# Tile loads issued as even and odd partitions, and one weight split moved ahead of another, in a retention and two-MLP kernel

## The chip, the cores and the metric

The kernel runs on one NeuronCore of a Trainium2 chip. The metric is the device time of one execution in microseconds (us), lower is better. A profiled execution gives the trace from which all rows below are read; its span runs from the first to the last instruction.

## The reference

Retention over 4 batches, 8 heads, 576 positions and head dimension 64, then two feed-forward blocks on the 2304 x 512 result, all in float32:

```python
scores = scale * np.matmul(q, k.transpose(0, 1, 3, 2))
ret = scores * Dmat[None, :, :, :]          # Dmat[h, i, j] = gamma[h] ** (i - j) for i >= j, else 0
attn_out = np.matmul(ret, v)
x = attn_out.transpose(0, 2, 1, 3).reshape(B * S, H * D)
...
h = x @ w_in;  x = np.maximum(h, 0.0) ** 2 @ w_out             # w_in 512 x 2048, w_out 2048 x 512
h = x @ w_in2; x = (h * np.clip(h + 3.0, 0.0, 6.0) / 6.0) @ w_out2
```

The four weight matrices come as 8-byte floats and are turned into 4-byte floats on the chip.

## The kernel before

**Retention.** The work is cut into ten units `u`: two pairs of batches, five blocks of positions each (four of 128, the last of 64). A unit of full width needs four tiles, two of queries and keys (`qkt`, from `in_qk`) and two of keys and values (`kvt`, from `in_kv`), each 128 partitions by 1024 floats, 512 KB. The last unit of a pair needs one tile from `in_qk_last` (512 KB) and two pieces of values of 128 KB, each 64 partitions wide: one goes to the lower 64 partitions of a tile, one to the upper (L271). Three pairs of tiles live in a buffer called `early`. So there are 16 + 16 whole tiles, two tiles from `in_qk_last` and four half-width pieces. Per unit, GpSimd (POOL) scales the keys (`scale_keys`, L283), TensorE (PE) makes scores (`aps`) and sums (`vps`, `sps`), VectorE (DVE) multiplies by the decay and writes the result into `xall` (L372).

**First feed-forward block.** For token group `pos` and chunk `c` of 128 hidden features, `emit_h` makes `hps` (24 matmuls where the group has 768 tokens, L439), ScalarE (ACT) and DVE make `g`, and `y_steps`, two chunks later (`LAG`), adds `g` times the chunk of w_out into `yps` and `ytail` (L497). A chunk of w_in reaches PE in three steps: load into `stage`, decode on ACT and DVE, and `split_in`, which makes a high part on ACT (L195) and a low part on POOL (L196) in a tile `win`. A chunk of w_out goes the same way into a tile `wo` (`split_out`). Each w_in chunk of this block is loaded in four pieces: 256 KB (L142), 128 KB (L144) and two of 64 KB (L145 and L146), the last two 64 partitions wide. The first two chunks of w_in are loaded between the tiles, chunks three to five and two chunks of w_out right behind the last tiles.

**Second block.** Its lines (L638 to L715) hold about half of PE's work and aren't touched.

**What sets the order.** The order in the program is written by hand, and each engine runs its instructions in that order. All loads of tiles and weights are issued by SyncE (SP), one after the other, in the order of the list `order` (built under `manual_schedule`); only the two loads of constants are issued by ACT. Eight completion semaphores, used in turn over SP's and ACT's loads, limit what is outstanding: a load waits until the load eight places ahead of it has landed. Tiles go to buffers that earlier tiles or steps leave free, so that some loads wait for PE or POOL as well.

The loop that the second part of the change touches runs over `i`, the pairs of `pos` and `c`: at `i` it emits `h` of chunk `i`, splits w_in of chunk `i + 2` (`split_in(*units[i + 2], ...)`, L931), splits w_out of chunk `i - 1` (`split_out(i - 1, ...)`, L933), and emits `y` of chunk `i - 2`.

Of the kernel before, what the change touches and what calls it, by code (L numbers as in the profile page):

```python
# [24 lines left out]
C = 128  # L25
# [50 lines left out]
def retention_moe_moe2(ctx, tc, qk, qk_last, kv, w_in, w_out, w_in2, w_out2, consts, out):  # L76

    nc = tc.nc
# [4 lines left out]
    NCH = DFF // 128  # L83
# [115 lines left out]
    def split_to(hi, lo, src, lo_engine):  # L199
        for f in split_parts(hi, lo, src, lo_engine):  # L200
            f()
# [8 lines left out]
    def unit(u):  # L210

        p, i = divmod(u, NTB)
        return 2 * p, i, min(C, S - C * i)
# [17 lines left out]
    def half(i):  # L231
        return slice(64 * i, 64 * i + 64)
# [3 lines left out]
    def space(u, k, which):  # L236

        b, i, n = unit(u)
        s = u // NTB * (2 * TILES + 1) + 2 * i + k
        if AHEAD <= s < AHEAD + WIDE:  # L240
            if not wide:
                wide.append(place("xr", [128, 2 * WIDE, 1024], F32, "early"))
            return wide[0][:, 2 * (s - AHEAD) + which]
        tags = TOKENS[s if s < AHEAD else (s - WIDE) % len(TOKENS)]
        name = ("qkt", "kvt")[which]
        if tags is None:
            return wop.tile([128, 1024], F32, tag="wo", name=name)
        return place(tags[which], [128, 1024], F32, name)

    def load_qk(u, k):  # L250
        b, i, n = unit(u)
        t = space(u, k, 0)
        if n == C:
            nc.sync.dma_start(out=t, in_=qk[b + k, i])
            data[u]["qk", k] = t.rearrange("p (e a t) -> p e a t", e=2, a=HP)
            return
        t = t.rearrange("p (b f) -> p b f", b=2)
        nc.sync.dma_start(out=t, in_=qk_last[b:b + 2].rearrange("b p e a t -> p b (e a t)"))
        for e in range(2):
            data[u]["qk", e] = t[:, e].rearrange("p (e a t) -> p e a t", e=2, a=HP)  # L260

    def load_kv(u, k):
        b, i, n = unit(u)
        t = space(u, k, 1)
        if n == C:
            t = t.rearrange("p (e h d) -> p e h d", e=2, h=H)
            nc.sync.dma_start(out=t, in_=kv[b + k, C * i:C * i + n])
            data[u]["k", k], data[u]["v", k] = t[:, 0], t[:, 1]
            return
        for e in range(2):  # L270
            nc.sync.dma_start(  # L271
                out=t[half(e), :H * D], in_=kv[b + e, C * i:, 1].rearrange("t h d -> t (h d)")
            )
        data[u]["v", 0] = t[:, :H * D].rearrange("p (h d) -> p h d", h=H)
# [112 lines left out]
    def split_x(pos, kk):  # L387
        t0, n = FIRST[pos]
        if pos == 0:
            if kk == 0:  # L390
                xtiles[0] = place("xr", [128, KD, 2, 768], F32R, "xring")
            hi, lo = (xtiles[0][:, kk, e] for e in range(2))
        elif (pos, kk) in ((3, 2),) or pos == 1:
            t = place("t7" if pos == 3 else ("x5", "x6", "t7", "ret")[kk], [128, 2, 512], F32R, "xown")
            hi, lo = (t[:, e] for e in range(2))
        else:
            if (pos, kk) == (2, 0):
                xtiles[2] = place("xr", [128, 2, 6, 512], F32R, "xring")
            slot = kk if pos == 2 else (4, 5, None, 0)[kk]
            hi, lo = (xtiles[2][:, e, slot] for e in range(2))  # L400
        xs[pos, kk] = hi, lo
        return split_parts(hi, lo, xall[:, kk, t0:t0 + n], nc.gpsimd if pos == 0 and kk in X_POOL else nc.vector)
# [8 lines left out]
    def wout_place():  # L411
        return wop.tile([128, 2, DM], F32R, tag="wo", name="wo")

    def split_out(c, lo_engine):
        w = wout_place()
        split_to(w[:, 0], w[:, 1], w32.pop((0, c, 1)), lo_engine)
        wouts[0, c] = w
# [12 lines left out]
    def emit_h(pos, c):  # L430
        w = wins.pop((pos, c))
        hs = []
        for k, (o, n) in enumerate(parts(pos)):
            own = pos == 0 or pos == 1 and c < LAG
            h = (bank(6 + (c % 2 if pos else k), [128, 512], "hps") if own else next_bank([128, 512], "hps"))[:, :n]
            m = 0
            for kk in range(KD):
                for wp, xp in PASSES:
                    nc.tensor.matmul(  # L439
                        out=h, lhsT=w[:, wp, kk * 128:kk * 128 + 128], rhs=xs[pos, kk][xp][:, o:o + n],  # L440
                        start=m == 0, stop=m == 3 * KD - 1,
                    )
                    m += 1
            hs.append(h)
        return hs
# [28 lines left out]
    def emit_g(pos, c, hs):  # L474
        relu, powers, low = g_steps(pos, c, hs)
        for k in range(len(relu)):
            relu[k]()
            powers[k]()
        for f in low:
            f()  # L480
# [270 lines left out]
    def next_load():  # L751

        turn["decoded"] += 1
        if coming and turn["decoded"] > 4:
            load_w(*coming.pop(0)[1:])

    with tc.manual_schedule():
# [88 lines left out]
        for u in range(UNITS):  # L846
# [6 lines left out]
            if u != 1:  # L853
                v = max(u - 1, 0)
                p = values(v)
# [7 lines left out]
        p = values(UNITS - 1)  # L863
# [16 lines left out]
        def opening(c, h, dec):  # L880

            relu, powers, low = g_steps(0, c, h)
            for f in dec[0]:
                f()
            next_load()
            for f in dec[1][:-1] if c == 0 else ():
                f()
            relu[0]()
            powers[0]()
            low[0]()  # L890
            if c == 0:
                dec[1][-1]()
                next_load()
            relu[1]()
            if c == 0:
                split_in(0, 2, nc.gpsimd)
            else:
                split_out(0, nc.vector)
            powers[1]()
            low[1]()  # L900

        for i, (pos, c) in enumerate(units):
            h = emit_h(pos, c)
            dec, due = due, []
            if i < 2:
                opening(i, h, dec)
                dec = []
            first = dec[:1]
            dec = dec[len(first):]
            for d in first:  # L910
                for f in d:
                    f()
                next_load()
            for d in dec:
                d.pop(0)()
            if pos and pos + 1 < len(FIRST) and c >= NCH - 3:
                for kk in ((0,), (1,), (2, 3))[c - NCH + 3]:
                    for f in split_x(pos + 1, kk):
                        f()
            if i > 1:  # L920
                emit_g(pos, c, h)
            for d in dec:
                for f in d:
                    f()
                next_load()
            if pos == 0 and c >= NCH - 3:
                for kk in ((0,), (1,), (2, 3))[c - NCH + 3]:
                    for f in split_x(pos + 1, kk):
                        f()
            if i and i + 2 < len(units):  # L930
                split_in(*units[i + 2], nc.gpsimd if i + 2 < NCH else nc.vector)  # L931
            if 2 <= i <= NCH:
                split_out(i - 1, nc.gpsimd)  # L933
            while halves and halves[0][0] <= i:
                d = decode(*halves.pop(0)[1:])
                d.pop(0)()
                due.append(d)
            if i >= LAG:
                for f in y_steps(*units[i - LAG]):
                    f()  # L940
                if i - LAG < NCH:
                    keep(("o", 0, i - LAG), wouts[units[i - LAG]].rearrange("p e n -> p (e n)"))
            if NCH <= i + 1 < len(units):
                load_out(0, *units[i + 1])
            if i in READY:
                owed += pace
                while ready and owed > ready[0][0] / 2:
                    cost, f = ready.pop(0)
                    f()
                    owed -= cost  # L950
            if pos == len(FIRST) - 1:
                if c == NCH - 5:
                    assert not ready
                    store_late()
                    load_left(0)
                if NCH - 5 <= c < NCH - 1:
                    for f in sums[2 * (c - NCH + 5):][:2]:
                        f()
                if c >= NCH - 3:
                    lows[c - NCH + 3]()  # L960
                if NCH - 4 <= c < NCH - 1:
                    highs[c - NCH + 4]()
# [13 lines left out]
        for k in range(total):  # L976
            j, p = divmod(k, NPAIR)
# [80 lines left out]
```

## Time and profile before

| | us |
|---|---|
| median of 3 runs (842.79 to 845.89) | 845.64 |
| the profiled execution's own time | 844.69 |
| its span | 842.9 |
| retention: from the start to the first `hps` matmul | 63.80 |
| PE busy in the whole span | 830.2 |

The span lies 1.8 us below the profiled execution's own time. In the page, engines are PE (matmuls), PEld (weight loads of TensorE), DVE, ACT, POOL and SP; SPq is SP's queue, where a load's row is its issue and not its transfer. "DMA share" is the mean busy share of the 16 DMA engines, and GB/s is what they moved.

### The profile page before, as it was taken

How to read it: one execution, taken by the hardware profiler on the slowest of the kernel's cores; microseconds unless marked ns; L12 is line 12 of the kernel's file. 1: busy time of each engine (PE TensorE's matmuls, PEld its weight loads, DVE VectorE, ACT ScalarE, POOL GpSimd, SP SyncE). 2: the span in 40 equal slices, each digit the busy share in tenths (PEclk: the TensorE clock that was granted, in tenths of full speed). 3: DMA queues.
4: the chain of work that ended last, by engine and by line, in shares of the span. 5: the costliest groups of instructions: out<-in, count | busy, mean ns of one | idle time of the engine just before them, and what ended most of it. 6: DMA issues, size and time to landing. Idle time of an engine off the chain costs nothing.

```text
span 842.9 us, 13274 instructions
## 1 busy us (share of the span) xinstructions
PE 830.2 (98%) x4932; PEld 721.6 (86%) x4932; DVE 524.6 (62%) x876; ACT 454.0 (54%) x847; POOL 142.9 (17%) x122
## 2 busy tenths in 40 slices
PE   8899999999999999999999999999999999999997
PEld 7788888888888888888888888898898889889896
DVE  5779777775777777687665644545644546534534
ACT  1247767676667877777665433345433345433332
POOL 2352323231432233333320000000000000000000
PEclk9999999999999999999999999999999999999999
DMA  9992556555778767877686464562864552854522
GB/s 361 366 324 70 189 177 199 177 191 190 262 265 311 250 240 264 307 277 251 225 290 246 171 218 163 176 211 89 310 227 163 190 197 89 331 208 160 205 95 76
DMA packets 67557, 183.47 MB, mean 218 GB/s; under 512 B 6818, under 2 KB 23586, under 8 KB 67492
## 3 DMA queue, kind: packets, MB, share of 16 engines
q1 hardware_dynamic: 66912, 181.82, 61.8%
q8 instruction: 39, 0.64, 0.3%
q10 hardware_dynamic: 580, 0.79, 0.3%
q14 instruction: 26, 0.21, 0.1%
HBM read 146.41 MB, written 36.18 MB: 217 GB/s over the span
## 4 chain that ended last, share of the span: by engine, by line
PE 85%; DMA 6%; DVE 2%; ACT 2%; issue 2%; POOL 1%; SPq 0%; ACTq 0%; DVEq 0%; POOLq 0%
PE yps L638 24%; PE hps L677 21%; PE hps L439 19%; PE yps L497 19%; DMA kvt<-in_kv_dram 4%; PE ytail L497 2%; DMA stage<-in_w_in_dram 2%; DMA cst<-in_consts_dram 1%; POOL wo L196 0%; POOL win L196 0%; DVE a L183 0%; ACT r L464 0%; ACT a L170 0%; ACT r L171 0%; DVE w L189 0%
## 5 line engine op out<-in xcount | busy, mean ns | idle before, releaser
L638 PE MATMUL yps<-wo,g 128*128 128x512 f32 x864 | 226.3, 394 | 0.0
L497 PE MATMUL yps<-g,wo 128*128 128x512 f32 x768 | 195.6, 392 | 1.0 <-POOL wo L196 1.0
L638 PEld LDWEIGHTS yps<-wo,g 128*128 128x128 f32 x864 | 159.7, 188 | 23.5 <-DVE g L692 0.3
L497 PEld LDWEIGHTS yps<-g,wo 128*128 128x128 f32 x768 | 140.0, 188 | 28.8 <-POOL wo L196 4.4
L439 PE MATMUL hps<-xring,win 128*128 128x512 f32 (+1 forms) x720 | 153.4, 362 | 0.9 <-DVE xall L372 0.9
L439 PEld LDWEIGHTS hps<-xring,win 128*128 128x128 f32 x720 | 123.2, 189 | 22.0 <-DVE xall L372 1.0
L677 PE MATMUL hps<-xlast,win 128*128 128x384 f32 x576 | 116.2, 336 | 0.0
L677 PEld LDWEIGHTS hps<-xlast,win 128*128 128x128 f32 x576 | 103.3, 188 | 8.8
L696 DVE TENSOR_TENSOR u<-hps,u 128x384 f32<-128x384 f32 x48 | 26.8, 558 | 107.3 <-PE hps L677 107.3
L468 DVE TENSOR_TENSOR g<-r,g 128x512 fp32r<-128x512 f32 x64 | 48.6, 760 | 69.5 <-ACT g L465 69.1
L677 PE MATMUL hps<-xop,win 128*128 128x384 f32 x432 | 87.2, 336 | 0.0
L461 ACT ACTIVATE r<-hps 128x512 f32<-128x512 f32 x80 | 43.9, 549 | 73.5 <-PE hps L439 73.4
L690 ACT ACTIVATE g<-c 128x384 fp32r<-128x384 f32 x72 | 37.8, 525 | 84.3 <-DVE c L689 84.3
L677 PEld LDWEIGHTS hps<-xop,win 128*128 128x128 f32 x432 | 77.5, 188 | 6.6
L688 ACT ACTIVATE v<-c,three 128x384 f32<-128x384 f32 x72 | 44.4, 617 | 32.7 <-DVE c L696 31.4
L439 PE MATMUL hps<-xown,win 128*128 128x512 f32 x240 | 59.7, 390 | 0.0
L195 ACT ACTIVATE win<-w 128x512 fp32r<-128x512 f32 x64 | 39.6, 619 | 26.8 <-DVE w L189 26.8
L715 ACT ACTIVATE c<-hps 128x384 f32<-128x384 f32 x24 | 11.8, 492 | 76.4 <-PE hps L677 76.4
L439 PEld LDWEIGHTS hps<-xown,win 128*128 128x128 f32 x240 | 44.9, 188 | 9.2
L174 DVE TENSOR_SCALAR a<-a 128x512 f32<-128x512 f32 x64 | 38.0, 594 | 23.0 <-ACT a L170 23.0
L464 ACT ACTIVATE r<-r 128x512 f32<-128x512 f32 x80 | 47.2, 590 | 2.5
L689 DVE SCALAR_TENSOR_TENSOR c<-v,c 128x384 f32<-128x384 f32 x72 | 40.0, 555 | 13.4 <-ACT v L688 13.4
(94 smaller groups left out, 983.0 us busy)
## 6 DMA issues: line engine op xcount, KB each, us to landing
wo<-kept SPq DMA_DIRECT2D x96, 512.0 KB, 5.0
win<-kept SPq DMA_DIRECT2D x72, 512.0 KB, 3.6
kept<-ready SPq DMA_DIRECT2D x40, 512.0 KB, 4.0
stage<-in_w_out_dram SPq DMA_DIRECT2D x32, 512.0 KB, 4.1
kept<-wo SPq DMA_DIRECT2D x16, 512.0 KB, 5.0
stage<-in_w_in_dram SPq DMA_DIRECT2D x16, 512.0 KB, 4.0
qkt<-in_qk_dram SPq DMA_DIRECT2D x13, 512.0 KB, 8.1
kvt<-in_kv_dram SPq DMA_DIRECT2D x13, 512.0 KB, 8.4
```

The source lines that it names most:

```text
L174: nc.vector.tensor_scalar(out=a, in0=a, scalar1=LEAST, scalar2=MOST, op0=ALU.max, op1=ALU.min)
L195: lambda: nc.scalar.activation(out=hi, in_=src, func=ACTF.Copy),
L439: nc.tensor.matmul(out=h, lhsT=w[:, wp, kk * 128:kk * 128 + 128], rhs=xs[pos, kk][xp][:, o:o + n], start=m == 0, stop=m == 3 * KD - 1,)
L461: relu.append(lambda r=r, h=hs[k]: nc.scalar.activation(out=r, in_=h, func=ACTF.Relu))
L464: nc.scalar.activation(out=r, in_=r, func=ACTF.Square)
L468: low.append(lambda r=r, hi=hi, lo=lo: nc.vector.tensor_tensor(out=lo, in0=r, in1=hi.bitcast(F32), op=ALU.subtract))
L497: nc.tensor.matmul(out=p, lhsT=w[:, wp, m * 128:m * 128 + 128], rhs=g[pos, c][k][:, gpart, :size], start=c == 0 and e == 0 and not (k and ...
L638: nc.tensor.matmul(out=p, lhsT=gt[m // 3][:, gpart, m % 3 * 128:][:, :128], rhs=w[:, wp], start=first and e == 0, stop=last and e == 2,)
L677: nc.tensor.matmul(out=to, lhsT=wl[k][:, half, wp, o], rhs=x[:, xp, f], start=first and m == 0, stop=last and m == 5, skip_group_check=True,)
L688: nc.scalar.activation(out=v, in_=c, func=ACTF.Relu, bias=three)
L689: nc.vector.scalar_tensor_tensor(out=c, in0=v, scalar=6.0, in1=c, op0=ALU.min, op1=ALU.mult)
L690: nc.scalar.activation(out=hi, in_=c, func=ACTF.Copy)
```

## The change

Every tile from `in_qk`, `in_kv` and `in_qk_last` is loaded by two loads of 64 partitions each, first the even partitions, then the odd ones (128 partitions by 4 KB become twice 64 by 4 KB). The half-width pieces of values and the weights are loaded as before. In the loop of the first block, at `i == 2`, the split of w_out chunk 1 is emitted ahead of the split of w_in chunk 4, where it stood behind it; from `i == 3` on the order is the old one.

```diff
         if n == C:
-            nc.sync.dma_start(out=t, in_=qk[b + k, i])
+            for e in range(2):
+                nc.sync.dma_start(out=t[e::2], in_=qk[b + k, i, e::2].rearrange("p e a t -> p (e a t)"))
             data[u]["qk", k] = t.rearrange("p (e a t) -> p e a t", e=2, a=HP)
             return
         t = t.rearrange("p (b f) -> p b f", b=2)
-        nc.sync.dma_start(out=t, in_=qk_last[b:b + 2].rearrange("b p e a t -> p b (e a t)"))
+        for e in range(2):
+            nc.sync.dma_start(
+                out=t[e::2], in_=qk_last[b:b + 2, e::2].rearrange("b p e a t -> p b (e a t)")
+            )
...
         if n == C:
+            for e in range(2):
+                nc.sync.dma_start(
+                    out=t[e::2], in_=kv[b + k, C * i + e:C * i + n:2].rearrange("p e h d -> p (e h d)")
+                )
             t = t.rearrange("p (e h d) -> p e h d", e=2, h=H)
-            nc.sync.dma_start(out=t, in_=kv[b + k, C * i:C * i + n])
...
+            if i == 2:
+                split_out(1, nc.gpsimd)
             if i and i + 2 < len(units):
                 split_in(*units[i + 2], nc.gpsimd if i + 2 < NCH else nc.vector)
-            if 2 <= i <= NCH:
+            if 3 <= i <= NCH:
                 split_out(i - 1, nc.gpsimd)
```

SP's queue at the start of the program, before; the names behind "waits" are the eight completion semaphores:

```order
L254 DMA qkt<-in_qk_dram 128x1024 x2
L267 DMA kvt<-in_kv_dram 128x1024 x2
L254 DMA qkt<-in_qk_dram 128x1024 x2
L254 DMA qkt<-in_qk_dram 128x1024 [waits DMAHW0_49]
L254 DMA early<-in_qk_dram 128x1024 [waits DMAHW1_49]
L267 DMA kvt<-in_kv_dram 128x1024 [waits DMAHW2_49]
```

The same place after the change:

```order
L255 DMA qkt<-in_qk_dram 64x1024 x4
L271 DMA kvt<-in_kv_dram 64x1024 x2
L271 DMA kvt<-in_kv_dram 64x1024 [waits DMAHW0_49]
L271 DMA kvt<-in_kv_dram 64x1024 [waits DMAHW1_49]
L255 DMA qkt<-in_qk_dram 64x1024 [waits DMAHW2_49]
```

Six loads are still issued before the first wait, but they are now three tiles instead of six, and the order of the tiles is the old one.

POOL's queue at the start of the first feed-forward block, before (`w_1002` holds w_in chunks 2 and 3, `w_1124` chunks 4 and 5):

```order
L196 TENSOR_TENSOR win<-w_1002,win 128x512 x2
L196 TENSOR_TENSOR win<-w_1124,win 128x512
L196 TENSOR_TENSOR wo<-wd,wo 128x512
L196 TENSOR_TENSOR win<-w_1124,win 128x512
L196 TENSOR_TENSOR wo<-wd,wo 128x512
```

The same place after the change, where the two buffers are called `w_1036` and `w_1158`:

```order
L196 TENSOR_TENSOR win<-w_1036,win 128x512 x2
L196 TENSOR_TENSOR wo<-wd,wo 128x512
L196 TENSOR_TENSOR win<-w_1158,win 128x512 x2
L196 TENSOR_TENSOR wo<-wd,wo 128x512
```

The low part of w_out chunk 1 has moved ahead of that of w_in chunk 4; on ACT, the two high parts have changed places in the same way.

## Rows read from the trace of the kernel before

**Rows 1.** The page's busy times of PE, and DMA in 40 equal slices of the span:

```profile
PE 830.2 (98%) x4932; PEld 721.6 (86%) x4932; DVE 524.6 (62%) x876; ACT 454.0 (54%) x847; POOL 142.9 (17%) x122
...
DMA  9992556555778767877686464562864552854522
GB/s 361 366 324 70 189 177 199 177 191 190 262 265 311 250 240 264 307 277 251 225 290 246 171 218 163 176 211 89 310 227 163 190 197 89 331 208 160 205 95 76
```

**Rows 2.** Waits up to 64 us: who for whom, us in total, times, longest:

```profile
POOL kvt L283 <- DMA kvt<-in_kv_dram: 27.7, 12, 8.0
```

**Rows 3.** The chain that ended last, up to 57 us (start, us, what):

```profile
6.56 11.17 DMA kvt<-in_kv_dram
...
49.50 7.08 DMA kvt<-in_kv_dram
```

**Rows 4.** The timeline behind the last tile: start, us, engine, line:

```profile
56.31 1.04 POOL L283 TENSOR_TENSOR kvt<-kvt,cst 128x512 f32<-128x512 f32 x1 [0.57 <-DMA kvt<-in_kv_dram]
...
63.80 13.02 PE L439 MATMUL hps<-xring,win 128*128 128x512 f32 x72 [0.88 <-DVE xall L372]
```

**Rows 5.** Stretches of retention; the last two numbers are DMA share and GB/s:

```profile
4.00:24.00 20.00, 18.50 (x330) 16.12 (x329) 13.40 (x23) 2.88 (x9) 7.80 (x7) 1.00 1.03 408
24.00:34.00 10.00, 8.21 (x218) 7.60 (x216) 4.38 (x9) 3.49 (x10) 3.06 (x4) 1.00 1.03 321
34.00:46.00 12.00, 10.78 (x208) 9.75 (x206) 11.94 (x22) 2.72 (x6) 4.70 (x4) 1.00 1.03 408
46.00:62.00 16.00, 15.03 (x355) 13.83 (x352) 11.19 (x17) 7.64 (x19) 10.35 (x9) 1.00 1.01 306
```

**Rows 6.** SP's queue where whole tiles are issued: start, us of one issue:

```profile
10.14 0.33 SPq L267 DMA_DIRECT2D kvt<-in_kv_dram  x1
11.41 0.33 SPq L267 DMA_DIRECT2D early<-in_kv_dram  x1
```

**Rows 7.** The 64-partition pieces of L271: their issue, and the last two's time to landing:

```profile
L271 SPq DMA_DIRECT2D kvt<-in_kv_dram x4: 471/471/471, 25.8 to 50.2; - x4
...
49.50 1.19 SPq L271 DMA_DIRECT2D kvt<-in_kv_dram  x2
...
kvt<-in_kv_dram SPq DMA_DIRECT2D x1, 128.0 KB, 7.1
...
kvt<-in_kv_dram SPq DMA_DIRECT2D x1, 128.0 KB, 6.8
```

**Rows 8.** The start: the first two stretches, and when the seventh SP load is issued:

```profile
0.00:2.00 2.00, 0.94 (x5) 0.69 (x6) 0.17 (x2) 0.25 (x1) 0.21 (x4) 1.00 0.10 18
2.00:4.00 2.00, 2.00 (x11) 1.40 (x10) 0.00 (x0) 1.03 (x1) 0.00 (x0) 1.00 0.86 296
...
5.16 0.33 SPq L254
```

**Rows 9.** The page's DMA issues, whole span: KB each, median us to landing:

```profile
stage<-in_w_in_dram SPq DMA_DIRECT2D x16, 256.0 KB, 2.7
```

**Rows 10.** PE, POOL and ACT around the wait for w_out chunk 1:

```profile
85.04 0.63 PE L497 MATMUL yps<-g,wo 128*128 128x512 f32 x2
86.53 0.51 PE L497 MATMUL yps<-g,wo 128*128 128x512 f32 x1 [0.86 <-POOL wo L196]
...
90.37 4.33 PE L439 MATMUL hps<-xring,win 128*128 128x512 f32 x24
...
83.75 1.30 POOL L196 TENSOR_TENSOR win<-w,win 128x512 fp32r<-128x512 f32 x1 [6.51 <-ACT win L195]
85.01 1.46 POOL L196 TENSOR_TENSOR wo<-wd,wo 128x512 fp32r<-128x512 f32 x1
...
80.57 0.42 ACT L465 ACTIVATE gtail<-r 128x256 fp32r<-128x256 f32 x1
83.04 0.63 ACT L195 ACTIVATE win<-w 128x512 fp32r<-128x512 f32 x1 [2.06 <-DVE w L189]
...
79.19 0.69 DVE L189 CUSTOM_DVE_ANT_0 wd<-a,r 128x1024 uint16<-128x1024 uint16 x1
```

**Rows 11.** PE's waits from 63.8 us to the end:

```profile
PE yps L497 <- POOL wo L196: 1.0, 2, 0.9
```

## The prediction

> **What bounds the kernel now.** I read the page first. PE is busy 830.2 of 842.9 us, and in the 40 slices the DMA engines are full only in the first three, at 361, 366 and 324 GB/s [rows 1]. So there are two stages: retention, up to 63.80 us, in which the loads set the pace, and the rest, in which PE does. Both parts of the change lie at or before 87 us, so I then read that beginning alone.
>
> The waits up to 64 us show who waits: POOL, which scales the keys of every tile, waits 27.7 us for tiles [rows 2]. The chain of waits says the same: up to 57 us it runs over loads, up to 11.17 and 7.08 us at a time [rows 3]. Behind the last tile the way is short and fixed: POOL scales its keys at 56.31, and the first `hps` matmul starts at 63.80, 7.5 us later [rows 4]. Once that matmul has started, PE hardly stops again: its only named waits to the end beside the one that starts it are 1.0 us on `wo` [rows 11]. So what the last tile's landing loses or gains goes through to the end nearly whole.
>
> How fast are the loads? In the stretches that move whole tiles almost alone (4 to 24 and 34 to 46 us) the DMA share is 1.03 and the rate 408 GB/s. In the two stretches between and behind them the share is as full (1.03 and 1.01) but the rate is 321 and 306 GB/s [rows 5]. The loads that stand in these two and not in the others are the half-width pieces of values, and the w_in chunks with their 1 KB rows and their two 64-partition pieces. A full share at a lower rate means that the engines aren't starved but that each packet takes longer. A whole tile takes 1.27 us: SP issues one each time one has landed, at 10.14 and 11.41 us [rows 6], and 524,288 bytes at 408 GB/s are 1.285 us.
>
> **The change part by part.**
>
> *Twice the issues.* 32 tiles and two from `in_qk_last` become 68 loads, 34 more. A 64-partition load takes SP 0.47 us to issue [rows 7], against 0.33 for a whole tile [rows 6]. Two halves are 0.94 us, below the 1.28 us that their bytes need, so SP still waits for landings and not the other way round: nothing, while that cover holds. If SP came to be the bound (an issue of 0.64 us or more) each tenth above would cost 68 x 0.1 = 6.8 us. SP has no other work in this stage; what queues behind its waits are the weight loads, which keep their places.
>
> *Half the bytes outstanding.* Eight halves are 2.1 MB, 5.1 us at 408 GB/s. A 256 KB load with little beside it lands 2.7 us after its issue [rows 9]. 5.1 is above 2.7, so in the steady stretches the engines don't run dry, and the tiles land in the old order at the old rate. The queue is shorter, but in a queue that is never empty the last byte comes when all bytes ahead of it have been moved; a shorter queue is worth nothing in itself.
>
> *The start.* Here the queue does run thin. Six halves are issued before the first wait, 1.57 MB or 3.9 us. Data starts at about 1.8 us (18 GB/s in the first 2 us) and the constants come beside it, so these bytes last to about 6 us. The seventh load is issued when the constants have landed, at 5.16 us [rows 8], and its data follows about 1.1 us behind its issue, as the first load's did (0.7 to 1.8). That is a gap of 0.3 to 0.6 us: I take +0.5.
>
> *What a 64-partition load costs.* This term decides. The trace has no load of every other partition; it has loads of 64 neighbouring ones. The last two pieces of L271 were issued at 49.50 and 50.22 (49.50 + 1.19 - 0.47) and landed 7.1 and 6.8 us later, at 56.6 and 57.0 [rows 7]: 0.45 us apart for 131,072 bytes, where 408 GB/s would give 0.32. That is a factor of 1.4 per byte. The stretches give a far worse one: they lose 10 x (1 - 321/408) = 2.1 and 16 x (1 - 306/408) = 4.0 us, with 384 and 640 KB of 64-partition loads in them. Charged to these bytes alone, 6.1 us on 1.05 MB make a factor of 3.4, but the 1 KB rows of w_in share the blame. From below, a load of every other partition may cost nothing more, since it goes to both halves of the tile and its packets are the same 4 KB; a gain per byte is excluded, because the whole tiles already run at a full share.
>
> The tiles are 34 x 524,288 = 17.8 MB, 43.7 us at 408 GB/s. So the ends are +0 (factor 1.0), +17.5 (1.4) and, if the stretches were right, over +100. The nearest rows are L271's, loads of 64 partitions that come one behind the other like these. But those fill one half of the partitions, and the even ones both halves, so part of what slows them should fall away; I take 1.3, that is +13.1 us. All of it lies on the path, since POOL already waits for every tile.
>
> [...]
>
> *The split moved.* PE waits 0.86 us in front of the third `yps` matmul of chunk 1 for the low part of its `wo`. POOL made that part at 85.01, behind the low part of w_in chunk 4 at 83.75, whose high part ACT could only start at 83.04, after 2.06 us of waiting for DVE [rows 10]. The decoded w_out chunk is ready at 79.19 + 0.69 = 79.9. With the new order ACT makes its high part behind `gtail` (81.0 to 81.6) and POOL its low part by 81.6 + 1.46 = 83.1, before PE asks for it, behind the two matmuls that start at 85.04. The w_in chunk now comes second, but ACT can't start it before 83.04 in either order and PE starts that chunk's `hps` only at 90.37 [rows 10]. So -0.9 us, and next in line is nothing that PE names [rows 11].
>
> **Sum.** 844.7 (the profiled execution's own time, 0.9 below the median) + 13.1 + 0.5 - 0.9 = 857.4 us.
>
> **The rivals.** *No price for the halves* (factor 1.0 to 1.05). For it: every DMA engine keeps 4 KB packets, each pair of halves covers the same partitions as the tile did, and the queue holds nearly twice what its latency needs. Against it: the only 64-partition loads in the trace are dear. It gives 844.7 + 0.5 - 0.9 = 844.3, and up to 846.5 at factor 1.05.
>
> *The slow stretches heal.* The 6.1 us that the two stretches lose could come from engines that are far apart: with eight whole tiles queued, one engine may write pieces of 64 partitions while another still writes whole tiles, and the two hinder each other. With half the bytes in the queue they stand closer together. For it: the share is full, so something inside the packets is slow. Against it: the tiles would then have to be free of that themselves, and the 1 KB rows stay. If two thirds of it heal: 844.3 - 4 = 840.3. This one ends faster, and decides as soon as more than about 3.8 us of the 6.1 come back.
>
> *Much slower.* Should the halves hinder each other as the pieces in the stretches do, the factor is 1.6 and more: +26 us, 870 or above. It needs the even and odd loads to collide all the time and not only at their ends.
>
> **How the numbers follow.** 0.5% of the median is 4.2 us, about what a measurement of this kernel can tell from no change. Halves that cost 1.1 to 1.55 (848 to 868): 0.43. Much slower: 0.07. No price: 0.38. Healing: 0.12. The likeliest is the first, at 857.4; its own range is 848 to 868. Since cases of both signs hold the chance, the range reaches over "no price" and to the lower end of its neighbour: 842 to 868, which leaves out some 0.09 below and 0.07 above. Faster by over 0.5% (below 841.4): 0.10. Within 0.5%: 0.40. Slower: 0.50.
>
> **What would show it.** Right: in the changed kernel the stretch from 4 to 24 us runs at 300 to 350 GB/s at a full DMA share, tiles land about 1.7 us apart instead of 1.28, and the first `hps` matmul starts near 76 us. Wrong toward "no price": 400 GB/s or more there, and the first `hps` matmul within 1 us of 63.8. Wrong toward healing: that matmul before 61 us, and over 350 GB/s in the stretches that hold the weight pieces. A DMA share clearly below 1 in the middle of a tile stretch would mean that the queue runs dry or that SP can't issue fast enough, so that a term I cost at nothing was the dear one. The second part is right if the wait on `wo` before `yps` of chunk 1 is gone; it is wrong if `hps` of chunk 4 waits for its `win` instead.

## The result, and the profile after

The changed kernel takes 848.12 us (median of 6 runs, 847.45 to 850.53); six runs of the kernel before on the same chip have a median of 843.89. The ratio is 1.0051, with a 95% interval of 1.0032 to 1.0071: 4.2 us slower. I had forecast 857.4, 12.7 us above the 844.7 from which I counted, so the sign was right and the size three times too large, and the reasons were mostly wrong too.

The profiled execution (850.53 us) is the slowest of the six. Its page, to be read beside [rows 1]:

```profile
PE 834.3 (98%) x4932; PEld 724.8 (85%) x4932; DVE 525.9 (62%) x876; ACT 454.0 (53%) x847; POOL 143.2 (17%) x122
...
DMA  8895565656578768876877465463764462864532
GB/s 326 282 313 157 174 198 174 198 183 215 206 265 300 252 244 296 300 259 232 287 236 272 161 215 190 143 223 110 273 253 169 168 215 88 308 225 162 193 105 75
```

Of the three slices that were full before, two no longer are. The same five stretches as in [rows 5], and one more, since retention now ends later (last two numbers: DMA share, GB/s; the number ahead of them is the granted clock):

```profile
4.00:24.00 20.00, 17.94 (x264) 15.15 (x261) 9.70 (x16) 2.52 (x9) 5.61 (x6) 0.83 0.98 366
24.00:34.00 10.00, 10.00 (x259) 9.54 (x254) 6.56 (x12) 3.33 (x11) 4.45 (x6) 1.00 0.84 270
34.00:46.00 12.00, 7.42 (x144) 6.43 (x136) 9.56 (x17) 1.44 (x4) 0.92 (x1) 1.00 0.90 294
46.00:62.00 16.00, 15.95 (x327) 14.80 (x327) 9.12 (x14) 6.03 (x16) 7.47 (x7) 0.89 0.90 305
62.00:70.00 8.00, 6.68 (x170) 5.54 (x163) 7.84 (x12) 3.63 (x10) 6.77 (x7) 1.00 1.00 282
```

This isn't the picture that I had forecast. I expected a full share at a lower rate, engines busy with dear packets. Here the share itself falls: 0.84 to 0.90 from 24 to 62 us, where every stretch had 1.01 to 1.03 before. Part of the engines wait for work. And where the share is full, they move halves as fast as they moved tiles:

```profile
10.00:16.00 6.00, 6.00 (x52) 4.50 (x54) 1.23 (x2) 0.60 (x1) 1.64 (x2) 0.53 1.01 406
16.00:22.00 6.00, 6.00 (x122) 5.81 (x119) 5.59 (x10) 1.14 (x4) 2.08 (x2) 1.00 1.02 397
```

Who keeps them waiting stands in SP's queue. First its timeline at the start (start, us, line, number of issues), then the issue times of the tile loads by line (shortest/median/longest in ns), after, and the line that answers to them in the kernel before:

```profile
3.27 2.51 SPq L271 DMA_DIRECT2D kvt<-in_kv_dram  x4
5.83 4.11 SPq L255 DMA_DIRECT2D qkt<-in_qk_dram  x6
```

```profile
L255 SPq DMA_DIRECT2D qkt<-in_qk_dram x26: 472/588/1484, 0.7 to 48.7; - x26
...
L271 SPq DMA_DIRECT2D early<-in_kv_dram x6: 472/597/2644, 18.2 to 23.3; - x6
```

```profile
L254 SPq DMA_DIRECT2D qkt<-in_qk_dram x13: 327/337/1096, 0.7 to 36.3; - x13
```

Four halves start within 5.83 - 3.27 = 2.56 us, 0.64 each. A tile costs SP 1.28 us, the time that the DMA engines need for it. So SP hardly waits for landings any more, as the first rows of SP's waits up to 62 us show (before, then after: who for whom, us in total, times, longest):

```profile
SPq L267 <- DMA kvt<-in_kv_dram: 5.3, 5, 2.1
SPq L254 <- DMA qkt<-in_qk_dram: 3.0, 4, 1.1
SPq L267 <- DMA qkt<-in_qk_dram: 2.7, 3, 0.9
```

```profile
SPq L271 <- DMA kvt<-in_kv_dram: 3.6, 3, 2.8
SPq L255 <- PE aps L329: 1.2, 1, 1.2
SPq L145 <- DMA qkt<-in_qk_dram: 1.2, 1, 1.2
SPq L255 <- PE sps L353: 0.7, 2, 0.4
```

Before, the three largest are waits for landings, 11.0 us; now the landings that SP waits for are few, and waits for PE (a buffer still in use) have joined them. Behind it all, POOL waits for tiles for 36.7 us in the first 66 us, 27.7 us in the first 64 before [rows 2], and PE's first `hps` matmul starts at 69.76 instead of 63.80 [rows 4]:

```profile
POOL kvt L290 <- DMA kvt<-in_kv_dram: 36.7, 12, 13.2
```

```profile
69.76 10.63 PE L446 MATMUL hps<-xring,win 128*128 128x512 f32 x55
```

Those 5.96 us are the whole of the longer span, 848.7 - 842.9 = 5.8 us, in this execution; the medians differ by 4.2. The second part of the change did what it says and gained nothing: chunk 1's `yps` doesn't wait any more, chunk 2's does, for longer than chunk 1's did [rows 10]:

```profile
99.57 0.63 PE L504 MATMUL yps<-g,wo 128*128 128x512 f32 x2
101.43 0.50 PE L504 MATMUL yps<-g,wo 128*128 128x512 f32 x1 [1.23 <-POOL wo L196]
```

One more thing stands in this trace. PE idled for lack of tiles, and twice its granted clock fell behind such a stretch: to 0.53 from 10 to 16 us (above), after it had idled 1.60 us in front of 8.31, and to 0.57 from 46 to 50, after 4 us in which it was busy for 0.94:

```profile
42.00:46.00 4.00, 0.94 (x16) 0.88 (x16) 2.02 (x3) 0.00 (x0) 0.92 (x1) 1.00 0.94 338
46.00:50.00 4.00, 3.97 (x56) 3.70 (x54) 1.29 (x2) 0.15 (x1) 1.17 (x2) 0.57 0.86 285
```

### The profile page after: what moved, and what is told of

Its sections match the earlier page's. It is cut to its first block, busy times and chain, and to the rows that moved or that the text cites. A ratio compares the mean times of both kernels' runs of the same rounds, so it can differ in the third digit from the quotient of the medians.

```text
span 848.7 us, 13334 instructions
## 1 busy us (share of the span) xinstructions
PE 834.3 (98%) x4932; PEld 724.8 (85%) x4932; DVE 525.9 (62%) x876; ACT 454.0 (53%) x847; POOL 143.2 (17%) x122
## 4 chain that ended last, share of the span: by engine, by line
PE 91%; DMA 3%; SPq 1%; issue 1%; DVE 1%; ACT 1%; POOL 1%; POOLq 0%; ACTq 0%; DVEq 0%
PE yps L645 24%; PE hps L446 21%; PE hps L684 21%; PE yps L504 20%; DMA kvt<-in_kv_dram 2%; PE ytail L504 2%; PE vps L345 1%; PE aps L329 1%; DMA qkt<-in_qk_dram 1%; PE sps L353 0%; DMA stage<-in_w_in_dram 0%; PE vps L361 0%; SPq L255 0%; DVE w L189 0%; DVE g L475 0%
## 5 line engine op out<-in xcount | busy, mean ns | idle before, releaser
L722 ACT ACTIVATE c<-hps 128x384 f32<-128x384 f32 x24 | 11.8, 492 | 76.5 <-PE hps L684 76.5
```

## The experiments

My theory after this reading (theory A in the expectations): a half load's bytes cost nothing, but its issue does. SP needs as long for a tile as the DMA engines do, so after any delay it can't get ahead again, and with half the bytes queued a delay reaches the engines sooner. The rivals: the shorter queue alone (theory B), a cost of 64-partition loads as such (theory C), the moved split, the clock. The kernels and what they gave (differences of medians in us, to the kernel before on the same chip):

| kernel | us | difference | ratio, 95% interval |
|---|---|---|---|
| split_alone | 844.92 | +0.2 | 0.9998 (0.9990 to 1.0006) |
| halves_alone | 848.51 | +3.8 | 1.0038 (1.0025 to 1.0051) |
| column_halves | 845.19 | +0.5 | 1.0009 (1.0001 to 1.0018) |
| short_queue | 846.37 | +1.7 | 1.0022 (1.0014 to 1.0031) |
| pause_eight | 844.68 | 0.0 | 0.9998 (0.9988 to 1.0008) |
| pause_whole | 846.12 | +1.6 | 1.0021 (1.0012 to 1.0030) |
| column_pause | 848.64 | +4.0 | 1.0048 (1.0036 to 1.0061) |
| quarters | 887.43 | +42.9 | 1.0510 (1.0485 to 1.0534) |
| contiguous_halves | 871.56 | +27.0 | 1.0320 (1.0295 to 1.0346) |
| late_halves | 846.10 | +1.4 | 1.0018 (1.0009 to 1.0026) |
| split_all | 845.04 | +0.5 | 1.0005 (0.9995 to 1.0014) |
| merged_last | 846.43 | +1.8 | 1.0022 (1.0014 to 1.0031) |

**Which part.** The two parts apart. `split_alone` is the kernel before with the diff's last piece only, `halves_alone` has the other two.

> Whole tile loads as before; only the moved w_out split of chunk 1. Theory (the split is worth nothing): the changed kernel waited 1.2 us for wo once, a chunk later, where the kernel before waited 1.0 us in two parts, so this one gives 843 to 845, ratio 0.999 to 1.001, with the wait for wo at the next chunk. Rival (the split costs part of the 4.2 us that the change lost): 845.5 us or more. Rival of the prediction: 0.9 us gained, 843.0.

> Even and odd halves as in the changed kernel; the two weight splits in their old order. If all of the loss is the loads': 847.5 to 849 us, ratio 1.004 to 1.006, retention's end at 68 to 70 us, the two waits for wo of 1.0 us together back. If the moved split has a part in it: at least 1.5 us less than the changed kernel.

The split alone is worth nothing, and the wait has moved to the next chunk:

```profile
95.81 0.50 PE L497 MATMUL yps<-g,wo 128*128 128x512 f32 x1 [1.25 <-POOL wo L196]
```

The halves alone lose 3.8 of the 4.2 us, and the intervals overlap widely: the loss is the loads'. This run's trace also clears the clock. It was granted in full through retention, and the first `hps` matmul was still 5.5 us late, in the slowest of five executions:

```profile
4.00:24.00 20.00, 17.03 (x284) 14.52 (x283) 10.51 (x18) 2.88 (x9) 4.85 (x6) 1.00 0.96 344
24.00:34.00 10.00, 9.31 (x231) 8.49 (x231) 5.47 (x11) 2.73 (x8) 4.90 (x6) 1.00 0.88 299
34.00:46.00 12.00, 8.74 (x172) 7.54 (x166) 9.70 (x17) 1.54 (x4) 1.45 (x2) 1.00 0.95 311
46.00:62.00 16.00, 14.74 (x317) 12.76 (x313) 11.18 (x18) 6.76 (x18) 7.30 (x6) 1.00 0.97 333
62.00:70.00 8.00, 6.82 (x147) 5.73 (x148) 5.20 (x10) 2.78 (x7) 6.28 (x6) 1.00 0.96 279
```

```profile
69.25 11.06 PE L446 MATMUL hps<-xring,win 128*128 128x512 f32 x57
```

**The shorter queue by itself.** `column_halves` cuts each tile by columns. It has as many loads of as many bytes as the change, but 128 partitions in each:

```diff
-            nc.sync.dma_start(out=t, in_=kv[b + k, C * i:C * i + n])
+            for e in range(2):
+                nc.sync.dma_start(out=t[:, e], in_=kv[b + k, C * i:C * i + n, e])
```

> Two loads for a tile again, 256 KB each, but each of 128 partitions by 2 KB: as many issues and as few bytes outstanding as in the changed kernel. Theory A (SP's issue time): a 128-partition issue took 0.33 to 0.47 us before, so a pair takes 0.7 to 0.9 us of the tile's 1.28, SP gets ahead again after each delay, and the time is 844 to 845.5, with the DMA share at 1.0 from 10 to 24 and from 34 to 46 us. Theory B (half the bytes outstanding run out, whatever an issue costs): 847.5 to 849 with the share falling under 0.9 in the same places as in the changed kernel. Theory C (a load of 64 partitions is itself slow): as A, and the loads' landings are then 1.28 us a tile.

`short_queue` loads whole tiles and sends a load of one element behind each, which takes up every second of the eight completion semaphores, and so of the eight places among the outstanding loads:

```diff
+    def dot():
+        nc.sync.dma_start(out=dots[:, spot[0]:spot[0] + 1], in_=consts[:1, :1])
+        spot[0] += 1
...
             nc.sync.dma_start(out=t, in_=qk[b + k, i])
+            dot()
```

> Whole tile loads with a one-element load behind each, which takes every second of the eight places in the queue: four tiles outstanding at most (half the bytes), one long issue per tile (0.33 to 0.47 us) and a small one (estimate 0.1 to 0.3). Theory A (issue time): SP is far from bound, 844 to 846. Theory B (the bytes outstanding): 847.5 to 849, with the DMA share under 0.9 in several stretches of two microseconds between 22 and 60 us.

The column halves lose 0.5 us, far from 3.8. Their issue is cheap, and the DMA share is full where the change left it at 0.84 and 0.90 (issue times in ns, shortest/median/longest; then two stretches):

```profile
L255 SPq DMA_DIRECT2D qkt<-in_qk_dram x26: 327/402/1664, 0.7 to 44.3; - x26
```

```profile
24.00:34.00 10.00, 8.96 (x232) 8.24 (x228) 4.92 (x10) 3.43 (x10) 3.55 (x5) 1.00 1.05 318
34.00:46.00 12.00, 10.46 (x199) 9.44 (x199) 11.54 (x21) 2.72 (x6) 3.27 (x3) 1.00 1.00 353
```

So theory B, the shorter queue as the whole cause, falls. The column halves do have a small price of their own per byte: from 10 to 20 us, where both kernels move tiles at a full share, their 2 KB rows go at 390 GB/s and the whole tiles of before at 412 (before, then `column_halves`):

```profile
10.00:20.00 10.00, 8.67 (x178) 8.19 (x177) 6.84 (x12) 1.46 (x6) 2.08 (x2) 1.00 1.03 412
```

```profile
10.00:20.00 10.00, 9.69 (x189) 9.12 (x190) 7.58 (x13) 1.74 (x5) 3.30 (x3) 1.00 1.06 390
```

But `short_queue` came out above the range that theory A gave it, with 1.7 us. A tile and its small load took SP 0.33 and 0.29 us:

```profile
10.90 0.33 SPq L275 DMA_DIRECT2D kvt<-in_kv_dram  x1
11.28 0.29 SPq L239 DMA_DIRECT2D dots<-in_consts_dram  x1
```

That is far from binding, so the queue has a part in the loss, or else the small loads have one of their own, which no run sets apart. Why four whole tiles outstanding should be worse than eight halves of the same bytes, these runs don't tell.

**SP's time by itself.** Whole tiles and the full queue again, but SP is kept busy: a number of semaphore increments, which nobody waits for, stand behind each tile load. Eight make a tile cost SP about 0.8 us, sixteen make it 1.32.

```diff
+    def pause():
+        for _ in range(16):
+            nc.sync.sem_inc(tick, 1)
...
             nc.sync.dma_start(out=t, in_=qk[b + k, i])
+            pause()
```

> Whole tile loads, all eight places of the queue for data (4 MB outstanding), but sixteen semaphore increments on SP behind each tile load, which delay nothing but SP. The trace of before has two such instructions on SP 0.055 to 0.075 us apart, so SP needs about 0.33 + 16 x 0.06 = 1.3 us for a tile, as much as two half loads (2 x 0.64). Theory A (SP's time is the loss): 847 to 849 us, retention's end 3 to 5 us later, DMA share under 0.95 in stretches behind each long issue. Rival (the loss needs small loads or a short queue): 844 to 845.5, since the queue holds as many bytes as before.

> Whole tile loads, eight semaphore increments on SP behind each: 0.33 + 8 x 0.061 = 0.82 us of SP for a tile that the DMA engines take 1.28 us for. Theory A with a threshold (SP's time costs nothing until it nears the engines' time): 844 to 845.2. If SP's time costs in proportion (half of the 1.6 to 1.8 us that sixteen cost): 845.3 to 845.6.

SP's timeline with sixteen: two loads in 1.64 us, and 17.17 - 14.53 = 2.64 us for the pair, 1.32 a tile.

```profile
14.53 1.64 SPq L259 DMA_DIRECT2D early<-in_qk_dram  x2
17.17 0.33 SPq L274 DMA_DIRECT2D kvt<-in_kv_dram  x1
```

At 0.8 us of SP for a tile the loss is 0.0, at 1.32 it is 1.6: no cost in proportion, but a threshold somewhere between the two, where the engines' own 1.28 lies too. And 1.32 is 0.04 more than 1.28, so that 34 x 0.04 = 1.4 of the 1.6 us may be SP as the plain bound. 1.6 is less than the 2.5 to 4.5 that theory A had promised. SP's time alone isn't the whole loss either.

**Both together.** `column_pause` is the column halves with five increments behind each, so that a half costs SP about what an even or odd one did:

> The halves by columns (128 partitions by 2 KB) with five semaphore increments on SP behind each, which took 0.061 us each in the run with sixteen of them: 0.33 + 0.31 = 0.64 us of SP for a half, what an even or odd half costs it, and as few bytes outstanding, but no load of 64 partitions. If SP's time and the short queue together are the whole loss: the sum of their own losses, 0.8 and 1.8 us, to the 3.8 us of the even and odd halves, so 847 to 849. If loads of 64 partitions lose time of their own: 844.5 to 846.

```profile
18.35 1.00 SPq L277 DMA_DIRECT2D kvt<-in_kv_dram  x2
19.69 1.00 SPq L277 DMA_DIRECT2D early<-in_kv_dram  x2
```

```profile
24.00:34.00 10.00, 8.87 (x235) 8.52 (x237) 5.07 (x10) 2.83 (x9) 5.15 (x6) 1.00 0.92 321
34.00:46.00 12.00, 9.50 (x170) 8.74 (x166) 9.21 (x17) 1.44 (x4) 2.09 (x2) 0.86 0.89 302
```

Two halves start in 19.69 - 18.35 = 1.34 us, 0.67 each, the share is down again as in the changed kernel, and the loss is 4.0 us, that of `halves_alone` (3.8). So a loss of this size needs no tile load of 64 partitions. The dose isn't quite the same: 0.67 is 0.03 more than an even or odd half costs SP, 68 x 0.03 = 2.0 us, but the engines, too, need 262,144 bytes / 390 GB/s = 0.67 us for a column half. In both kernels SP has nothing to spare; that the two losses are equal to a microsecond isn't shown.

The parts lost 0.5 and 1.6 us alone (0.8 and 1.8 by the ratios, as in the expectation) and 4.0 together. By the ratios the excess over the sum is some 1.5 us, and known to about as much. So that the two causes support each other, since a slow SP can't fill the queue again and a short queue can't cover a slow SP, is my reading and likely, but not shown; the runs show that the two together make a loss of the right size.

**What the delays are.** The traces show two kinds, which my theory had not named. In all fourteen traces together, 64 of SP's issues that start before 110 us took over 0.85 us. During 63 of them the queue that the page calls `q8 instruction` had one of its 16 KB packets on the way, but during only 125 of the 1392 shorter ones. The longest is the one of 2.64 us in the changed kernel (SP's timeline; then that queue from 23.4 to 25.7 us: packets, MB, share):

```profile
23.26 2.64 SPq L271 DMA_DIRECT2D early<-in_kv_dram  x1
```

```profile
q8 instruction: 1, 0.02, 6.1%
```

The kernel before has such an issue too, of 1.10 us at 28.27, but it issues a tile in 0.33 us and has the rest of 1.28 to make up for it. What the packet has to do with SP is not shown. The other kind is a load whose last part comes late. SP's longest wait for a landing after the change, 2.8 us up to 44.94, is for the half issued at 37.04: fourteen of its sixteen landing records are in by 42.34, the last comes at 44.92. All that time eight halves were outstanding, and from 42 to 43 us the DMA share was 0.83: some engines stood idle while that part was on its way. That a single engine lagged behind the others is my reading; the landing records don't name engines.

**More of the same dose.** Four loads of 32 partitions for a tile (`t[e::4]`):

> Four loads for a tile, every fourth partition each (32 partitions, 128 KB); the weight splits in the old order. Theory A with an issue of 0.47 to 0.6 us whatever its partitions: 4 x 0.55 = 2.2 us of SP for a tile of 1.28, so SP sets the pace: 34 tiles x 0.9 = 31 us more, 870 to 880, with a DMA share near 0.6. If the issue's time falls with the partitions (0.3 us): 848 to 850. If only the bytes outstanding count (a quarter of before): 850 to 856, with SP waiting for landings.

```profile
L271 SPq DMA_DIRECT2D kvt<-in_kv_dram x52: 527/592/1335, 5.8 to 99.0; - x52
```

```profile
4.00:24.00 20.00, 13.26 (x152) 10.25 (x150) 7.57 (x13) 1.74 (x5) 2.56 (x3) 0.87 0.63 198
```

An issue of 32 partitions takes as long as one of 64, 0.59 us, so 4 x 0.64 = 2.56 us for a tile and 34 x (2.56 - 1.28) = 43.5 us more; 42.9 were measured, in two runs. My expectation had been lower by its 0.55 us for an issue. Here SP is the bound outright.

**Which 64 partitions.** The halves as partitions 0 to 63 and 64 to 127 (`t[64 * e:64 * e + 64]`):

> The halves are partitions 0 to 63 and 64 to 127 in place of even and odd ones; the weight splits in the old order. If a load's partitions don't matter to its speed: as even and odd halves alone, 847.5 to 849.5. If the 64 neighbours take 1.3 times as long per byte, the term that the prediction put on even and odd ones: 43.7 us x 0.3 = 13 us more, 858 or so, with stretches at a share of 1.0 and 300 GB/s.

```profile
4.00:24.00 20.00, 16.83 (x168) 13.19 (x165) 8.49 (x16) 1.74 (x5) 2.99 (x3) 0.88 1.03 233
```

27 us slower, twice what the dear one of my two cases gave, and now with the picture that I had forecast for the change: a full share, 233 GB/s instead of 408. That is a factor of 1.75 per byte for 64 neighbours, against 1.0 for even and odd partitions. At 233 GB/s the 17.8 MB need 76.5 us instead of 43.7, and 27 of these 33 us reach the end; where the other 6 went stays open.

**Start or later.** The first eight tiles whole, halves from the third unit on (`if u < 2` keeps the old call):

> Whole loads for the eight tiles of the first two units, even and odd halves from there on; the weight splits in the old order. If the loss is made at the start, where the first kvt landed 1.8 us later: 844.5 to 846. If it is made behind the delays later on, when SP can't catch up: 847 to 848.5.

```profile
4.00:24.00 20.00, 18.88 (x336) 16.46 (x335) 13.67 (x23) 2.89 (x9) 7.64 (x7) 1.00 1.01 398
24.00:34.00 10.00, 9.42 (x228) 8.52 (x224) 5.65 (x13) 3.55 (x10) 3.24 (x5) 1.00 0.96 311
34.00:46.00 12.00, 8.94 (x178) 7.95 (x176) 9.19 (x16) 2.72 (x6) 3.19 (x3) 1.00 0.88 302
```

It loses 1.4 us, between the two expectations. So some 3.8 - 1.4 = 2.4 us (each of the two known to about 1) are lost because the first eight tiles are halved, while SP sends them at the very pace at which they are moved, and 1.4 later on, where the share falls to 0.88.

**Two attempts at a faster kernel.** `split_all` puts each w_out split ahead of the w_in split, whole tiles otherwise:

```diff
+            if 2 <= i <= NCH:
+                split_out(i - 1, nc.gpsimd)
             if i and i + 2 < len(units):
                 split_in(*units[i + 2], nc.gpsimd if i + 2 < NCH else nc.vector)
-            if 2 <= i <= NCH:
-                split_out(i - 1, nc.gpsimd)
```

> Whole tile loads; the w_out split goes ahead of the w_in split for every chunk from the first on, not for one. If the wait for wo only moves a chunk on each time: 844 to 845, no difference. If it goes altogether and hps doesn't come to wait for win: 1.0 us less, 843 to 844. If hps waits for win in its place: 845 to 847.

```profile
PE yps L497 <- POOL wo L196: 0.5, 1, 0.5
```

Half of the 1.0 us of waiting is gone from this trace, but the time isn't shorter by anything that can be measured. (This trace is of the slowest of twelve executions, 847.06 us. Its first `hps` matmul starts at 66.17 us with the old loads, behind a granted clock of 0.93 from 46 to 62 us: single traces of retention differ by some 2 us, and the losses here rest on the medians.) `merged_last` joins the two contiguous half loads of the last values into one:

```diff
-        for e in range(2):
-            nc.sync.dma_start(
-                out=t[half(e), :H * D], in_=kv[b + e, C * i:, 1].rearrange("t h d -> t (h d)")
-            )
+        nc.sync.dma_start(
+            out=t[:, :H * D], in_=kv[b:b + 2, C * i:, 1].rearrange("b t h d -> b t (h d)")
+        )
```

> Whole tile loads; the two loads of the last values, 64 neighbouring partitions each, are one load of 128 partitions. The contiguous halves landed 1.13 us apart for 256 KB where even and odd ones took 0.64: so each of the two loads of 128 KB takes about 0.57 us and the merged one 0.64 for both, 0.5 us less for each of the two pairs, and two issues of 0.47 us less. If the transfers bound the retention: 1.0 us less, 843.2 to 844. If not: no difference.

```profile
63.75 1.09 PE L337 MATMUL vps<-ret,kvt 128*64 128x128 f32 x16 [2.35 <-DMA kvt<-in_kv_dram]
```

It is slower, by 1.8 us, and PE waits for just this load. Issued at 52.43 us, it had landed only at 63.61, 11.2 us later, where the two pieces of before took 7.1 and 6.8 [rows 7]; the first merged load, issued at 25.69, landed at 37.05, with just two landing records at its end (36.88 and 37.05). The tile issued behind that one, at 27.43, was late in part: of its sixteen landing records fourteen are in by 33.9 us, the last two come at 38.0 and 38.1, some 4 us later. My reading is that the merged load lay on two DMA engines alone and put these two behind the others. As an estimate, half of its 262,144 bytes at a sixteenth of 408 GB/s takes 5.1 us, where a sixteenth of them takes 0.64: 4.5 us more. The trace doesn't show which engine moved what, so the cause isn't shown.

## Why the prediction was right or wrong

**What bounds the kernel: right.** The late loads went through to the end nearly whole (5.96 us at the first `hps` matmul, 5.8 in the span).

**Twice the issues: wrong, and the step that mattered.** I costed it at nothing, with 0.47 us for an issue, and named the condition: no harm unless an issue takes 0.64. It took 0.64, and together with the shorter queue that is enough for the loss of 3.8 us of `halves_alone`, as `column_pause` (4.0) shows. The row that I used [rows 7] is of issues 0.72 us apart; back to back, one took 0.57 to 0.60 and 0.04 to the next. The cover of 1.28 us that hid the term was gone to the last tenth. `pause_eight` and `pause_whole` (0.0 and 1.6 us) show that a threshold lies between 0.8 and 1.32 us a tile, and `quarters` (42.9 us, where the issues add up to 43.5) that beyond it, as the prediction had it, every tenth is paid at every issue.

**Half the bytes outstanding: wrong in part.** I compared 5.1 us of queue with a latency of 2.7 and called it enough. Alone it costs 0.5 (`column_halves`) to 1.7 us (`short_queue`). What I left out are the delays: single issues that are held up, one here for 2.64 us, and loads whose last part comes late, one here 2.6 us (44.92 - 42.34) behind fourteen of its sixteen records. As I read it, the queue must cover the latency and such a delay, and with a slow SP it does not refill in between.

**The start: a loss as forecast, but too small and for another reason.** 0.5 us forecast; halving the first eight tiles accounts for about 2.4 (3.8 less the 1.4 of `late_halves`). I had the seventh load wait for the constants until 5.16 us. It didn't: the four halves from 3.27 on, numbers five to eight, went out without a pause, the seventh at 3.27 + 2 x 0.64 = 4.55. But SP sent them no faster than they are moved, and the first tile of keys and values had landed at 9.41 us instead of 7.57.

**A 64-partition load's cost per byte: wrong.** This term made the forecast: 13.1 us, factor 1.3. It measured nothing: 397 to 406 GB/s at a full share, against 408. The nearest rows were of 64 neighbours, and even and odd partitions don't behave like them: neighbours went at 233 GB/s. The price of neighbours was itself read too low, 1.4 where `contiguous_halves` shows 1.75. The 1.3 was a value between that 1.4 and no price, and no run shows it: the runs have 1.75 for neighbours and 1.0 for every other partition. Why the two differ isn't shown.

**The split moved: the wait went as said, the gain did not come.** The step "next in line is nothing that PE names" failed. POOL's work had only changed places: chunk 2's `wo` was now late by 1.2 us in place of chunk 1's 0.9.

**The rivals.** "No price for the halves" was right about the bytes and wrong about the time, because the issue wasn't priced in it. Nothing healed: the two stretches in question got no faster (270 and 305 GB/s, 321 and 306 before). That rival's 840.3 is counted from the profiled execution and its 3.8 us from the median; from the former it is 2.9. So the time lay inside the range by luck, for a reason that was in none of the cases, only in the last sentences of the prediction: a share below 1 in a tile stretch would mean that the queue runs dry or that SP can't issue fast enough. That is what the trace shows.

## What to carry to other kernels

Before a load is cut in two, set the time of its issues, back to back, against the time that the engines need for its bytes, here 1.28 us a tile: about 0.8 us of SP's time were free (`pause_eight`, 0.0 us), 1.28 with half the bytes queued weren't (`halves_alone`, +3.8 us), and at 2.56 every issue was paid in full (`quarters`, +42.9 us). Half the bytes in the queue cost 0.5 us here (`column_halves`), a slow SP 1.6 (`pause_whole`), and both 4.0 (`column_pause`), so look twice at a change that takes from both. And if a tile must be cut, cut the columns (128 partitions; +0.5 us here, with a rate of 390 GB/s instead of 412) or take every other partition (397 to 406 GB/s, but 0.64 us an issue; +3.8 us), not neighbours (233 GB/s; +27 us).

## What the runs showed of the hardware

- The issue of a load on SP took 0.33 us for 128 partitions and 0.47 for 64; back to back it took 0.43 for 128 (two in 0.90 us at 1.66 us in the kernel before) and 0.59 for 64 or 32: fewer partitions made it longer, not shorter.
- 63 of the 64 longest issues on SP (over 0.85 us) fell together with a 16 KB packet of the queue `q8 instruction`, and 125 of the 1392 shorter ones.
- Even and odd partitions: 397 to 406 GB/s at a full share (1.02 and 1.01). 64 neighbours: 233 at 1.03.
- A semaphore increment on SP took 0.062 us of its time ((1.32 - 0.33)/16).
- Rows of 2 KB in 128 partitions: 390 GB/s at a full share; rows of 4 KB: 412.
- The merged load of `merged_last`, 128 partitions and 256 KB from two batches, landed 11.2 us after its issue; the two pieces of before took 7.1 and 6.8.
